# Attention and a SwiGLU FFN in one kernel: values loaded ahead of two q/k transfers, product pieces from unit 8, and a gate step in a small PSUM bank

## The chip, the cores and the metric

The kernel runs on one core of a Trainium2 chip. TensorE does matrix products into PSUM, ScalarE the exponentials, tanh and some evictions, VectorE the other element-wise work, GpSimd (POOL) issues most transfers and makes some copies, SyncE (SP) issues the rest. The metric is the device time of one execution in microseconds (us); below it is the median of eight executions.

## The reference, cut to what matters

Attention over 8 batches of 12 heads, 448 positions, head size 64. Its output, as 3584 tokens of 768, goes through a gated FFN of 1536 hidden units.

```python
scores = np.matmul(q, k.transpose(0, 1, 3, 2)) / np.sqrt(64)
scores = scores - np.max(scores, axis=-1, keepdims=True)
attn = np.exp(scores)
attn = attn / (np.sum(attn, axis=-1, keepdims=True) + 1e-09)
x = np.matmul(attn, v)            # then (B, S, H*D), flattened to 3584 x 768
g = x @ w_gate
silu = g * (1.0 / (1.0 + np.exp(-g)))
out = (silu * (x @ w_val)) @ w_out
```

## The kernel before

The unit of the attention is a pair of heads: 48 pairs, six to a batch. Each pair is cut into four chunks of 112 key positions. `qk` (line 215) makes the scores of one chunk for both heads in one two-bank tile of the pool `ps_s`, and ScalarE's exponential (line 227) takes them to the tile E. `pv_chunk` (line 237) adds one chunk's product of E and the values to the accumulator `acc`; the values carry a column of ones, so that the sum of the exponentials comes with it. After the fourth chunk VectorE takes the reciprocal (line 265) and scales into `xt` (line 266). `turn_x` (line 283) transposes `xt` into X, which the FFN reads: on TensorE for the pairs below 12 (lines 293 and 297, then VectorE's copy, line 304), by DMA for the later ones. For pairs 1 to 10 `prep` transposes q and k on TensorE (line 207), with VectorE's copies (lines 208 and 211); later pairs go through POOL copies (line 166) and DMA transposes.

PSUM has eight banks. `ps_s` has three tiles of two banks, used in turn for the scores, for the transposes of pairs below 8, and for the FFN's gate product `gp`. `ps_f` has two tiles of one bank, called small banks here, used in turn for `acc`, the transposes of pairs from 8 on, the turns of x from pair 6 on, the FFN's value product `vp`, its output product `op`, and dummies. A new tile takes the buffer that was allotted longest ago and waits until the last reader of that buffer is done.

An FFN step (`ffn1_steps`, line 313) is six matmuls of the gate weights, six of the value weights, a tanh (line 334), and two VectorE steps: line 339 reads `sg` and `gp`, line 342 reads `vp` and writes `hts`. Twelve steps make a block of tokens; then `ffn2_steps` multiplies with the output weights (line 365) and ScalarE evicts (line 372).

The order of the work on each engine is written by hand. The first stage (line 476) has 24 units u, one chunk of scores each, for pairs 0 to 5. A unit may also turn q and k (`prep`), run a dummy matmul, copy values, emit loads (`wq`), turn x, and run pieces: a piece is one `pv_chunk` of the list `pieces`, allowed where its chunk number is at most u - 3, and here only from unit 12 on. Pairs 6 to 47 follow in visits (line 528) of two, later three chunks of scores. A visit may have products of a whole pair (`todo`); one with scores but without products is called bare. Then come FFN steps, as many as a budget gives. Before them a flag is set in bare visits that have no output step to run first: `val_first` (lines 568 and 584) makes the next FFN step run its value product ahead of its gate product.

Each engine runs its instructions in order. Transfers on the POOL queue wait for the landing of the eighth transfer before them. Values are loaded for three pairs in one transfer at first (`load_v`, line 132; 336 KB), then copied to a layout with the column of ones (`copy_v`, line 139): on POOL for pairs 0 to 5, on VectorE after that. `load_qk16` (line 118) loads q and k as 16-bit numbers, two pairs at a time from pair 4 on.

Of the kernel before, what the change touches and what calls it, by code (L numbers as in the profile page):

```python
# [10 lines left out]
FP32 = mybir.dt.float32  # L11
# [7 lines left out]
GP = 3  # L19
# [3 lines left out]
FIRST = 6  # L23
# [4 lines left out]
NV = 6  # L28
VS = 6
# [4 lines left out]
def kernel(  # L34
# [10 lines left out]
    nc = tc.nc  # L45
    B, H, S, D = q.shape
# [3 lines left out]
    NC = S // P  # L50
# [29 lines left out]
    ps_s = ctx.enter_context(tc.tile_pool(name="ps_s", bufs=3, space=PSUM))  # L80
    ps_f = ctx.enter_context(tc.tile_pool(name="ps_f", bufs=2, space=PSUM))
# [3 lines left out]
    Vts = [consts.tile([P, 2, NC, D + 2], FP16, name=f"vo{i}") for i in range(NV)]  # L85
    vraw = consts.tile([P, VS, 2, NC, D], FP16, name="vraw")
# [7 lines left out]
    def wslice(kind, fb, cb):  # L94
        i, off = divmod(fb * 128, DF // 4)
        return wgv[kind, i][:, cb, ds(off, 128)]
# [7 lines left out]
    def dummy(n):  # L104
        wp = ps_f.tile([128, 512], FP32, tag="f", name="wp")
        for _ in range(n):
            nc.tensor.matmul(wp[:], lhsT=warm[:, 0:128], rhs=warm[:], start=True, stop=True)
# [10 lines left out]
    def load_qk16(pr, n=2):  # L118
        h0 = 2 * (pr % 2) if pr >= 14 else 0
        if h0 == 0:  # L120
            q16 = raws.tile([P, 4, NC, D], FP16, tag="rq", bufs=RB, name="q16")
            k16 = raws.tile([P, 4, NC, D], FP16, tag="rk", bufs=RB, name="k16")
            pairbuf[:] = [q16, k16]
        q16, k16 = pairbuf
        for dst, src in ((q16, q), (k16, k)):
            flat = src.rearrange("b h s d -> (b h) s d")[2 * pr : 2 * pr + 2 * n]
            nc.gpsimd.dma_start(dst[:, ds(h0, 2 * n)], flat.rearrange("h (p c) d -> p h (c d)", c=NC))  # L127
        for i in range(n):
            h = h0 + 2 * i
            raw[pr + i] = (q16[:, h : h + 2], k16[:, h : h + 2])  # L130

    def load_v(pr, n=1):
        b, h = divmod(2 * pr, H)
        nc.gpsimd.dma_start(  # L134
            vraw[:, ds(pr % VS, n)].rearrange("p r h c d -> p (r h) (c d)"),
            v[b, h : h + 2 * n].rearrange("h (p c) d -> p h (c d)", c=NC),
        )

    def copy_v(pr):
        eng = nc.gpsimd if pr < FIRST else nc.vector  # L140
        eng.tensor_copy(Vts[pr % NV][:, :, :, 0:D], vraw[:, pr % VS])  # L141

    def load_w(kind, i):
        if kind == "o":
# [134 lines left out]
    def pv(pr):  # L279
        for c in range(NC):  # L280
            pv_chunk(pr, c)
# [26 lines left out]
        )  # L308
        nc.sync.dma_start_transpose(dst[:, 0:D].rearrange("p (j q) -> p j q", j=1), xt[0:D, 3])

    val_first = [False]

    def ffn1_steps(kk, c0, n, hts):
        for fb in range(NFB):
            gp = vp = None

            def group(kind, dst):
                for cb in range(NCB):
                    nc.tensor.matmul(  # L319
                        dst[:, 0:n],  # L320
                        lhsT=wslice(kind, fb, cb),
                        rhs=X[kk][:, cb, ds(c0, n)],
                        start=(cb == 0),
                        stop=(cb == NCB - 1),
                    )

            if val_first[0]:
                val_first[0] = False
                vp = ps_f.tile([128, 512], FP32, tag="f", name="vp")
                group("v", vp)  # L330
            gp = ps_s.tile([128, 2, 512], FP32, tag="s", name="gp")[:, 0]
            group("g", gp)
            sg = fp.tile([128, 512], FP32, tag="sg")
            nc.scalar.activation(sg[:, 0:n], gp[:, 0:n], AF.Tanh, scale=0.5)  # L334
            if vp is None:
                vp = ps_f.tile([128, 512], FP32, tag="f", name="vp")
                group("v", vp)
            t1 = fp.tile([128, 512], FP32, tag="t1")
            nc.vector.scalar_tensor_tensor(  # L339
                t1[:, 0:n], sg[:, 0:n], 1.0, gp[:, 0:n], ALU.add, ALU.mult  # L340
            )
            nc.vector.scalar_tensor_tensor(  # L342
                hts[:, fb, 0:n], t1[:, 0:n], 0.5 * HS, vp[:, 0:n], ALU.mult, ALU.mult
            )
            yield
# [53 lines left out]
    with tc.manual_schedule():  # L399
# [7 lines left out]
        make_identity(nc, ident)  # L407
        load_qk16(2, 1)
        load_qk16(3, 1)
        load_qk16(4)  # L410
        load_v(0, GP)
        load_v(3, GP)
        dummy(7)
        prep(0)()
# [12 lines left out]
        def emit(item):  # L427
            if item[0] == "qk":
                load_qk16(*item[1:])
            elif item[0] == "V":  # L430
                load_v(item[1] * GP, GP)
            else:
                load_w(*item)
# [31 lines left out]
        def left():  # L465
            return sum(2 * t for _, t in fvq) + sum(t for _, t in oq)

        def share(total, at, n):
            return (at + 1) * total // n - at * total // n

        pieces = [(p, c) for p in range(FIRST) for c in range(NC)]

        def piece():
            pv_chunk(*pieces.pop(0))

        for u in range(FIRST * NC):
            pr, c = divmod(u, NC)
            qk(pr, c)
            if u == 1:
                dummy(1)  # L480
                turn()
                dummy(1)
            elif u == 3:
                dummy(2)
            elif u == 4:
                prep(2)()
            elif u >= 6 and c == 2:
                prep(pr + 2)()
            if u in (5, 7, 8, 9, 11):
                dummy(1)  # L490
            if c == 1:
                if pr in (1, 3):
                    for p in range(3):
                        copy_v(3 * (pr // 2) + p)
                for w in wq.pop(pr, []):
                    emit(w)
            if u in (15, 17, 19, 21):
                turn_x((u - 15) // 2)
            for _ in range(2):
                if u >= 12 and pieces[0][0] * NC + pieces[0][1] <= u - 3:  # L500
                    piece()

        queue = []
# [24 lines left out]
        for x, (chunks, todo) in enumerate(plan):  # L528
            for pr, c in chunks:
                qk(pr, c)  # L530
            end = min([y for y in adds if y > x] + [len(plan) + 1])
            if x == 0:
                piece()
                turn_x(4)
                piece()
                piece()
                turn_x(5)
                add_block(0, end)
            for p0 in vcopies.get(x, []):
                copy_v(p0)  # L540
            entered = [pr for pr, c in chunks if c == 0]
            for pr in entered:
                if NPE <= pr + 3 < NPAIR:
                    prep(pr + 3)
                if 14 <= pr + LA < NPAIR:
                    load_qk16(pr + LA, 1)
                if 12 <= pr + 3 < NPAIR:
                    load_v(pr + 3)
            for pr, c in chunks:
                if c == 2 and pr < NPE - 2:  # L550
                    prep(pr + 2)()
            if x in adds and x > 0:
                add_block(adds[x], end - x)
            for _, p0 in todo:
                pv(p0)
                if p0 < XPE:
                    turns.append(p0)
                else:
                    turn_x(p0)
            for pr in entered:  # L560
                for w in wq.pop(pr, []):
                    emit(w)
            bare = not todo and bool(chunks)
            if adds[max(y for y in adds if y <= x)] < 2:
                if bare and oq and not fvq:
                    carry -= run_o()
                elif bare:
                    val_first[0] = True
                carry = run_budget(left() / (end - x) + carry)
            else:  # L570
                at, n = count["at"], count["visits"]
                no = share(count["o"], at, n)
                nf = 1
                if no and count["more"] > 0:
                    o_left = sum(1 for y in range(at, n) if share(count["o"], y, n))
                    extra = -(-count["more"] // o_left)
                    nf += extra
                    count["more"] -= extra
                count["at"] += 1
                if bare and no:  # L580
                    run_o()
                    no -= 1
                elif bare:
                    val_first[0] = True
                for y in range(nf):
                    if fvq:
                        run_fv()
                for _ in range(no):
                    run_o()
            while turns:  # L590
                turn_x(turns.pop(0))
# [39 lines left out]
```

The softmax here doesn't subtract the row's maximum and nothing guards it: scores larger than these inputs give would overflow.

## Time and profile before

| what | value |
|---|---|
| median of 8 executions | 456.94 us (456.41 to 457.5) |
| profiled execution, device time | 457.12 us |
| its span, first to last instruction | 455.3 us |
| TensorE busy | 444.6 us |
| ScalarE, VectorE, POOL busy | 238.9, 200.4, 141.8 us |
| read from HBM, written | 47.19 MB, 11.01 MB |
| the FFN's first matmul starts | 33.10 us |

The chain that ended last is 92% TensorE: output product 24%, gate 24%, value 24%, probability products 10%, scores 8%. In the timeline a row gives start, duration, engine, line, operation, what is written and read, shapes and count; brackets give the idle time of that engine before the row and what ended it. Matmul rows overlap at their ends, because matmuls are pipelined, so distances between starts are better measures of what a group costs than durations. Line numbers are those of the kernel before. The waits list sums the same idle times by who waited for whom.

### The profile page before, as it was taken

Reading aid. Unit: us, or ns where it says so; the run is one execution under the profiler, and the core shown is the slowest. Engines: PE = TensorE matmul, PEld = TensorE weight load, DVE = VectorE, ACT = ScalarE, POOL = GpSimd, SP = SyncE. Lnnn points to the kernel's source line nnn. Section 1 sums busy time; section 2 is a strip of 40 time slices with the busy share of each in tenths; the row PEclk is TensorE's granted clock in tenths of the full one; section 3 lists DMA queues with packets and bytes.
Section 4 is the critical chain, followed back from the end, with each engine's and each line's share of the span. In section 5 each row is a group of like instructions: output and inputs, shape, how many; then the busy total and the mean of one; then the engine's idle time right before and its main releaser. Section 6 shows DMA issues by size and latency. Waiting matters only on the chain.

```text
span 455.3 us, 9850 instructions
## 1 busy us (share of the span) xinstructions
PE 444.6 (98%) x4009; PEld 247.8 (54%) x4009; DVE 200.4 (44%) x450; ACT 238.9 (52%) x350; POOL 141.8 (31%) x228
## 2 busy tenths in 40 slices
PE   8989999999999999999999999999999999999997
PEld 3555555645455656545455565555555556644464
DVE  3455653356563534363453544444355444245400
ACT  6865476765654546644556455654654644222222
POOL 8664805926344315251332503441100000000000
PEclk9999999999999999999999999999999999999999
DMA  9999999999685739784766837983423102110033
GB/s 130 197 200 202 184 179 161 188 199 120 97 105 85 108 76 149 109 118 93 122 81 106 132 70 125 141 94 68 71 61 77 46 13 79 47 36 0 1 106 104
DMA packets 104942, 48.72 MB, mean 107 GB/s; under 512 B 59584, under 2 KB 101440, under 8 KB 104896
## 3 DMA queue, kind: packets, MB, share of 16 engines
q0 software_dynamic: 43296, 23.37, 41.4%
q1 hardware_dynamic: 61504, 24.66, 27.3%
q8 instruction: 31, 0.51, 0.5%
q14 instruction: 15, 0.12, 0.1%
q10 hardware_dynamic: 96, 0.05, 0.0%
HBM read 47.19 MB, written 11.01 MB: 128 GB/s over the span
## 4 chain that ended last, share of the span: by engine, by line
PE 92%; DMA 3%; POOL 2%; DVE 1%; ACT 1%; issue 1%; POOLq 0%; DVEq 0%
PE op L365 24%; PE gp L319 24%; PE vp L319 24%; PE acc L245 8%; PE s L219 8%; DMA wg<-in_moe_w_gate_dram 3%; PE acc L253 2%; POOL q L127 1%; DVE t L339 1%; POOL k L127 1%; ACT sg L334 1%; PE tp L207 0%; ACT E L227 0%; POOL vraw L134 0%; PE acc L293 0%
## 5 line engine op out<-in xcount | busy, mean ns | idle before, releaser
L227 ACT ACTIVATE E<-s 112x896 f16<-112x896 f32 x192 | 162.4, 921 | 27.3 <-PE s L219 27.0
L319 PE MATMUL vp<-X,wv 128*128 128x384 f16 (+1 forms) x576 | 124.7, 353 | 0.0
L319 PE MATMUL gp<-X,wg 128*128 128x384 f16 (+1 forms) x576 | 124.5, 352 | 0.0
L365 PE MATMUL op<-wo,hts 128*128 128x384 f16 (+1 forms) x684 | 116.0, 323 | 0.0
L339 DVE SCALAR_TENSOR_TENSOR t<-sg,gp 128x384 f32<-128x384 f32 (+1 forms) x96 | 59.6, 621 | 123.4 <-ACT sg L334 123.3
L334 ACT ACTIVATE sg<-gp 128x384 f32<-128x384 f32 (+1 forms) x96 | 52.5, 547 | 90.5 <-PE gp L319 89.4
L365 PEld LDWEIGHTS <-hts 128*128 128x128 f16 x684 | 65.5, 98 | 45.9 <-issue 3.9
L319 PEld LDWEIGHTS <-wv 128*128 128x128 f16 x576 | 55.9, 98 | 52.9 <-issue 1.1
L319 PEld LDWEIGHTS <-wg 128*128 128x128 f16 x576 | 53.5, 98 | 45.3
L372 ACT ACTIVATE osb<-op 128x384 f32<-128x384 f32 (+1 forms) x57 | 27.8, 487 | 92.4 <-PE op L365 88.3
L166 POOL COPY qk<-q 112x512 f16<-112x512 f16 x37 | 23.0, 621 | 133.8 <-DMA qkT<-qk 132.3
L342 DVE SCALAR_TENSOR_TENSOR hts<-t,vp 128x384 f16<-128x384 f32 (+1 forms) x96 | 59.6, 620 | 10.8 <-PE acc L253 0.5
L245 PEld LDWEIGHTS <-E 112*128 112x128 f16 x1152 | 46.2, 97 | 17.1 <-issue 15.9
L219 PE MATMUL s<-qkT 64*128 64x448 f16 x384 | 51.2, 353 | 4.1 <-DVE t L339 3.1
L245 PE MATMUL acc<-vo,E 112*128 112x65 f16 x1152 | 52.6, 193 | 1.1 <-POOL vo L141 1.1
L253 PE MATMUL acc<-vo,E 112*128 112x65 f16 x384 | 42.9, 193 | 0.0
L265 DVE RECIPROCAL R<-acc 128x7 f32<-128x7 f32 x48 | 9.8, 205 | 73.7 <-PE acc L253 73.7
L134 POOL DMA_DIRECT2D vraw<-in_v_dram x40 | 26.7, 669 | 28.7 <-DVE vo L141 16.1
L219 PEld LDWEIGHTS <-qkT 64*128 64x128 f16 x384 | 15.2, 94 | 31.4 <-issue 24.6
L127 POOL DMA_DIRECT2D k<-in_k_dram x42 | 27.9, 664 | 9.6 <-PE gp L319 8.1
L127 POOL DMA_DIRECT2D q<-in_q_dram x42 | 28.1, 669 | 2.5 <-PE s L219 1.0
L266 DVE TENSOR_TENSOR xt<-acc,R 128x384 f16<-128x384 f32 (+1 forms) x48 | 27.5, 574 | 1.7
(43 smaller groups left out, 155.1 us busy)
## 6 DMA issues: line engine op xcount, KB each, us to landing
q<-in_q_dram POOLq DMA_DIRECT2D x37, 112.0 KB, 3.9
k<-in_k_dram POOLq DMA_DIRECT2D x37, 112.0 KB, 4.5
vraw<-in_v_dram POOLq DMA_DIRECT2D x36, 112.0 KB, 4.4
out_dram<-osb SPq DMA_DIRECT2D x7, 336.0 KB, 3.2
wg<-in_moe_w_gate_dram POOLq DMA_DIRECT2D x8, 288.0 KB, 11.2
wv<-in_moe_w_val_dram POOLq DMA_DIRECT2D x8, 288.0 KB, 11.7
wo<-in_moe_w_out_dram POOLq DMA_DIRECT2D x2, 1152.0 KB, 22.5
out_dram<-osb SPq DMA_DIRECT2D x8, 288.0 KB, 3.8
```

The costliest lines, as they stand in the source:

```text
L127: nc.gpsimd.dma_start(dst[:, ds(h0, 2 * n)], flat.rearrange("h (p c) d -> p h (c d)", c=NC))
L219: nc.tensor.matmul(s[:, hx, 0:S], lhsT=t[ts(hx, 64), c * P : c * P + 128], rhs=t[ts(hx, 64), ds(S + (1 - hx) * D, S)], start=True, stop=True,)
L227: nc.scalar.activation(e[:, :, 0:S], s[0:P, :, 0:S], AF.Exp, scale=sm_scale)
L245: nc.tensor.matmul(a7[:, 2 * j + hx], lhsT=e[:, ds(c * EB + 9 * hx + 2 * j, 2)].rearrange("p b x -> p (b x)"), rhs=vo[:, hx, c, 0 : D + 1] ...
L253: nc.tensor.matmul(a7[:, 6], lhsT=e[:, ds(c * EB + 6 + hx, 2)].rearrange("p b x -> p (b x)"), rhs=vo[:, hx, c, 0 : D + 1], start=False, st ...
L266: nc.vector.tensor_tensor(xt[:].rearrange("p j (h d) -> p (j h) d", h=2)[:, 0:n], a7[:, 0:n, 0:D], r[:, 0:n].unsqueeze(2).to_broadcast([12 ...
L319: nc.tensor.matmul(dst[:, 0:n], lhsT=wslice(kind, fb, cb), rhs=X[kk][:, cb, ds(c0, n)], start=(cb == 0), stop=(cb == NCB - 1),)
L334: nc.scalar.activation(sg[:, 0:n], gp[:, 0:n], AF.Tanh, scale=0.5)
L339: nc.vector.scalar_tensor_tensor(t1[:, 0:n], sg[:, 0:n], 1.0, gp[:, 0:n], ALU.add, ALU.mult)
L342: nc.vector.scalar_tensor_tensor(hts[:, fb, 0:n], t1[:, 0:n], 0.5 * HS, vp[:, 0:n], ALU.mult, ALU.mult)
L365: nc.tensor.matmul(op[:, 0:w], lhsT=hts[:, fb, ts(ch, 128)], rhs=wo[oh][:, fb, ds(m0 - oh * OH, w)], start=(fb == 0), stop=(fb == NFB - 1),)
L372: nc.scalar.activation(osb[:, ds(m0, w)], op[:, 0:w], AF.Copy, scale=1.0 / HS)
```

## The change

Values of pairs 0 to 2 are loaded before q and k of pairs 4 and 5. All copies of values run on VectorE; those of pairs 0 to 2 are in unit 6 (after its transposes), of pairs 3 to 5 in unit 14, where both sets stood on POOL in units 5 and 13. Dummies are left in units 5, 6 and 7. Pieces may run from unit 8 on; a unit with a transpose set (c == 2) or a turn of x runs one piece, others up to two. The turns of x for pairs 0 to 3 move from units 15, 17, 19, 21 to 11, 15, 17, 20. In the first visit the turn of pair 4 stands before all remaining pieces rather than after one of them.

In the bare visits the flag, now `gate_small`, no longer puts the value product first. Instead the gate product runs first as in other steps, but in a small bank of `ps_f` rather than in a tile of `ps_s`.

```diff
     def copy_v(pr):
-        eng = nc.gpsimd if pr < FIRST else nc.vector
-        eng.tensor_copy(Vts[pr % NV][:, :, :, 0:D], vraw[:, pr % VS])
+        nc.vector.tensor_copy(Vts[pr % NV][:, :, :, 0:D], vraw[:, pr % VS])
...
-            if val_first[0]:
-                val_first[0] = False
-                vp = ps_f.tile([128, 512], FP32, tag="f", name="vp")
-                group("v", vp)
-            gp = ps_s.tile([128, 2, 512], FP32, tag="s", name="gp")[:, 0]
+            if gate_small[0]:
+                gate_small[0] = False
+                gp = ps_f.tile([128, 512], FP32, tag="f", name="gp")
+            else:
+                gp = ps_s.tile([128, 2, 512], FP32, tag="s", name="gp")[:, 0]
             group("g", gp)
             sg = fp.tile([128, 512], FP32, tag="sg")
             nc.scalar.activation(sg[:, 0:n], gp[:, 0:n], AF.Tanh, scale=0.5)
-            if vp is None:
-                vp = ps_f.tile([128, 512], FP32, tag="f", name="vp")
-                group("v", vp)
+            vp = ps_f.tile([128, 512], FP32, tag="f", name="vp")
+            group("v", vp)
...
+        load_v(0, GP)
         load_qk16(4)
-        load_v(0, GP)
         load_v(3, GP)
...
+        XAT = (11, 15, 17, 20)
...
-            if u in (5, 7, 8, 9, 11):
+            if u in (5, 6, 7):
                 dummy(1)
+            if u in (6, 14):
+                for p in range(3):
+                    copy_v(u // 8 * 3 + p)
             if c == 1:
-                if pr in (1, 3):
-                    for p in range(3):
-                        copy_v(3 * (pr // 2) + p)
                 for w in wq.pop(pr, []):
                     emit(w)
-            if u in (15, 17, 19, 21):
-                turn_x((u - 15) // 2)
-            for _ in range(2):
-                if u >= 12 and pieces[0][0] * NC + pieces[0][1] <= u - 3:
+            if u in XAT:
+                turn_x(XAT.index(u))
+            for _ in range(1 if c == 2 or u in XAT else 2):
+                if u >= 8 and pieces[0][0] * NC + pieces[0][1] <= u - 3:
                     piece()
...
             if x == 0:
-                piece()
                 turn_x(4)
-                piece()
-                piece()
+                while pieces:
+                    piece()
                 turn_x(5)
...
-                    val_first[0] = True
+                    gate_small[0] = True
```

More of the change, by code (lines that the diff above doesn't have):

```diff
@@ L309, in turn_x @@
         nc.sync.dma_start_transpose(dst[:, 0:D].rearrange("p (j q) -> p j q", j=1), xt[0:D, 3])
-    val_first = [False]
+    gate_small = [False]
     def ffn1_steps(kk, c0, n, hts):
         for fb in range(NFB):
-            gp = vp = None
             def group(kind, dst):
@@ L583 @@
                 elif bare:
-                    val_first[0] = True
+                    gate_small[0] = True
                 for y in range(nf):
```

## The prediction

> **What bounds the kernel now.** I read the page's busy line, then the waits, then the timeline of each engine around the places that the waits name.
>
> ```profile
> PE 444.6 (98%) x4009; PEld 247.8 (54%) x4009; DVE 200.4 (44%) x450; ACT 238.9 (52%) x350; POOL 141.8 (31%) x228
> PEclk9999999999999999999999999999999999999999
> ```
> ```profile
> PE s L219 <- DVE t L339: 3.1, 4, 0.9
> PE acc L245 <- POOL vo L141: 1.1, 2, 1.0
> PE acc L293 <- DVE xt L266: 1.0, 1, 1.0
> ```
>
> TensorE is busy 98% of the span. Time can only come from its gaps or from instructions it no longer has. The gaps named are 3.1 us of score products waiting for a gate bank (line 339 frees it), and about 2 us in the first stage. After 123 us the waits show no TensorE gap, so whatever is gained or lost before that reaches the end one for one.
>
> The four gaps, and the second FFN visit with what VectorE does meanwhile (start, duration, engine):
>
> ```profile
> 38.17 1.14 PE L319 MATMUL vp<-X,wv 128*128 128x384 f16 x6
> 39.14 1.14 PE L319 MATMUL gp<-X,wg 128*128 128x384 f16 x6
> 40.21 0.55 PE L219 MATMUL s<-qkT 64*128 64x448 f16 x4
> ...
> 50.40 0.36 PE L219 MATMUL s<-qkT 64*128 64x448 f16 x2 [0.68 <-DVE t L339]
> ...
> 60.46 0.37 PE L219 MATMUL s<-qkT 64*128 64x448 f16 x2 [0.61 <-DVE t L339]
> 60.76 0.35 PE L245 MATMUL acc<-vo,E 112*128 112x65 f16 x6
> ...
> 100.19 0.37 PE L219 MATMUL s<-qkT 64*128 64x448 f16 x2 [0.92 <-DVE t L339]
> 100.49 0.35 PE L245 MATMUL acc<-vo,E 112*128 112x65 f16 x6
> ```
> ```profile
> 38.73 0.29 DVE L141 COPY vo<-vraw 112x512 f16<-112x512 f16 x1 [0.61 <-DMA vraw<-in_v_dram]
> 38.94 0.62 DVE L208 COPY qkT<-tp 128x896 f16<-128x896 f16 x1
> 39.47 0.18 DVE L211 COPY qkT<-tp 128x64 f16<-128x64 f16 x1
> ...
> 46.99 0.72 DVE L141 COPY vo<-vraw 112x512 f16<-112x512 f16 x1
> ```
>
> At 38.73 VectorE had stood 0.61 us for the values of pair 6, and pair 8's turned q and k (lines 208, 211) stood behind that copy until 39.65. Nobody was hurt then: the next user of that bank came at 40.70.
>
> The values of pair 6 and the queue that brings them:
>
> ```profile
> 28.11 0.77 POOL L134 DMA_DIRECT2D vraw<-in_v_dram  x1 [0.42 <-issue]
> vraw<-in_v_dram POOLq DMA_DIRECT2D x1, 336.0 KB, 10.5
> 20.00:24.00 4.00, 3.30 (x69) 2.35 (x66) 3.19 (x8) 2.96 (x4) 2.59 (x4) 1.00 1.32 203
> 32.00:36.00 4.00, 3.33 (x23) 2.06 (x24) 1.46 (x3) 0.75 (x2) 2.18 (x4) 1.00 1.44 197
> ```
>
> Issued at 28.11, landed 10.5 later, at 38.6. The last two lines are four-microsecond stretches: busy time of TensorE, its weight loads, VectorE, ScalarE and POOL, then granted clock, DMA share and GB/s. The queue moves 195 to 203 GB/s in every 4 us stretch from 12 to 44 us, so a landing there is a matter of bytes ahead of it, not of when it is issued. The change swaps two transfers early on and adds none: pair 6 stays at 38.6.
>
> **Part 1: first stage (values first, VectorE copies, pieces from unit 8, fewer dummies).** The last transfer ahead of the swapped ones lands at 10.8 (k of pair 3, issued 5.25). The two value loads then took 1.8 and 2.3 us (landings 13.6, 15.4, 17.7), so values of pairs 0 to 2 come near 12.8 and k of pairs 4 and 5 near 15.4, where values came before. Six copies leave POOL (0.61 each) and cost VectorE 0.28 each where nothing disturbs them. TensorE per unit, from the starts in the timeline: scores 0.29, a lone piece 0.35, two pieces 0.57, a transpose set 0.52, a turn of x 0.42. Unit 8 starts at 12.3 as before (a score bank sets it), its pieces at about 13.1 with the copy; unit 10 stands for k until 15.4; unit 12 starts near 17.1 where before it was 15.55, but with six pieces and one turn done. Units 12 to 23 then hold 3 x 0.87 (two pieces) + 3 x 1.16 (transposes and a piece) + 3 x 1.06 (a turn and a piece) + 3 x 0.64 = 11.2, ending at 28.3 against 29.9. The tail (scores, turn 4, three pieces, normalisation, turn 5) keeps its 0.95 us stall before turn 5, merely elsewhere, and the FFN starts at about 31.7 instead of 33.1: 1.4 us earlier. The two lost dummies (0.3 each) lie in the stretch that the score bank sets, and are worth nothing alone.
>
> **Part 2: the second FFN visit eats it.** The bare visits (no probability products) run value first before, with gate in the three-deep score banks. Now gate takes a small bank, then value the other. The small banks are two and rotate: in this visit the transposes of pair 8 take one, gate the other, and value needs the transposes' bank back. That is line 211's end, 39.65, fixed by the landing at 38.6. Before, value took the older bank and gate a score bank, so neither waited. Now value starts at 39.70, however early TensorE arrives (37.7, after gate), and everything else on TensorE queues behind it. The next scores start a group and its tail later, 39.70 + 1.07 = 40.77 against 40.21: **+0.56**, and the 1.4 us are gone. The stage's result therefore doesn't matter over a wide range: it would have to end 0.56 us later than before to add anything, and no earlier end helps.
>
> **Part 3: the other bare visits.** Now the third score product needs only an exponential of the visit before. Its ungapped start is two pitches of 0.19 after the first.
>
> Visit at 47: the third score pair could start at 49.54 instead of 50.40, worth 0.86. Against it: value waits for the transposes of pair 9, whose copies ended at 48.32 on VectorE while value would start at 48.09: 0.28. That copy stood behind a value copy that took 0.72 (46.99) where the same copy takes 0.28 elsewhere (57.50), with POOL writing transfers until 47.59 and then copying:
>
> ```profile
> 45.54 2.05 POOL L154 DMA_DIRECT2D wo<-in_moe_w_out_dram  x2 [1.19 <-issue]
> 47.57 0.63 POOL L166 COPY qk<-q 112x512 f16<-112x512 f16 x1
> 48.12 0.63 POOL L166 COPY qk<-k 112x512 f16<-112x512 f16 x1
> ```
>
> With TensorE 0.56 later this copy comes at 47.55 and meets the POOL copies. Bounds of the wait: 0 if it takes 0.28; 1.1 if it stands until 48.75. Nearest is the row's own 0.28; I take 0.40. Net **-0.46**.
>
> Visit at 57: the scores flow, but the accumulator now needs the gate's bank, freed by line 339. The tanh stands behind three exponentials in both versions, so line 339 ends at 60.41 as before; the accumulator starts at 60.46 against 60.76: **-0.30**. The wait has moved, not gone.
>
> Visits at 96 and 118: gate is now done before the exponentials are, so the tanh follows them at once: 95.81 + 2.43 = 98.24, tanh 0.60, line 339 (0.69) from 98.87 to 99.56, accumulator at 99.61 against 100.49: **-0.88**. The same steps from 118.42 give 122.22 against 123.15: **-0.93**.
>
> Sum: +0.56 - 0.46 - 0.30 - 0.88 - 0.93 = -2.0. The profiled execution took 457.12 (span 455.3 and 1.8 around it), so 455.1; it stands 0.18 over the median of the eight, so **454.9**. Unknowns: pair 6's landing, one for one, up to one transfer of 1.14 us either way (26.4 to 27.6, values that pair with a 224 KB load); the 0.40, from 0 to 1.1.
>
> A rule that speaks against the change: the Trainium skill, "SBUF — State Buffer", section "SBUF: two separate sides", says that VectorE's fast copies and GpSimd lock each other out of a shared pair of ports for a whole instruction, and that transfers issued from GpSimd suffer because their descriptors can't be written. The 0.72 row agrees in kind. Six more such copies on VectorE would lock some 1.7 us, and were pair 6 as much later the time would be 456.6 by an estimate from that page; by the queue's steady rate, none of it.
>
> **The rivals.**
> *The gain of the first stage arrives* (faster). It needs pair 6 by 36.7, or value not to depend on it. Then -1.4 replaces +0.56: -3.97, **453.0**. For it: most of the edit is made there. Against: the steady 200 GB/s.
> *The wait takes the place of the one removed* (same). If the accumulator stands for the value's bank (line 342) rather than the gate's, then 60.51 + 0.55 gives 61.11 (+0.35), and 0.10 + 0.69 after line 339 gives 100.40 and 123.01 (-0.09, -0.14): sum +0.22, **457.2**. For it: in the visit at 47 the accumulator does follow the value's bank. Against: the banks rotate, and elsewhere the older one is the gate's.
> *TensorE's clock falls in units 8 to 12* (slower). Dummies go while TensorE waits for values at unit 8 and for k at unit 10. Place: the 15.2 us of work of units 8 to 23. It decides only beyond 2.0 us of slack before 39.70, 2.0 of later gains and 0.9: a mean clock under 15.2 / 20.1 = 0.76. At 0.65 it costs 8.2, **461**. Against: the stretches at 20 and 32 us hold gaps of 0.97 and 0.96 and show 1.00. The Trainium skill, "TensorE: Matmul & The Clock Gate", section "What's actually happening", has the clock halve only after an idle window of some 3.4 us; halving all units would give 468 by that page, and the rows show no such idleness.
>
> **How the numbers follow.** Forecast 0.66, with its own range 453.8 to 456.1; faster rival 0.12; same rival 0.12; slower 0.10. Half of the same rival and the slower one are left out by 453.0 to 456.5. A measurement can tell 0.2%, 0.9 us: faster means under 456.03, slower over 457.85. Of the forecast's 0.66 some 0.03 falls within: faster 0.63 + 0.12 = 0.75, same 0.12 + 0.03 - 0.01 = 0.14, slower 0.11.
>
> **What would show it.** Right: FFN starts near 31.7; a TensorE gap of about 2 us before value at 39.7, released by VectorE's copy of pair 8's transposes; a landing of pair 6 at 38.6; a gap of about 0.55 before the accumulator at 60; gaps under 0.3 near 99 and 122; no score product waiting for line 339 at the four places. Wrong: pair 6 landing elsewhere; a score product still waiting at those places; a clock below 1.00; a new wait after 123 us.

## The result, and the profile after

The changed kernel takes 454.16 us (median of 11, 453.76 to 455.38) where the kernel before took 456.85 beside it: ratio 0.9939, 95% interval 0.9930 to 0.9948, that is 2.4 to 3.2 us less. The forecast was 2.0 less. The profiled execution took 453.57, 0.6 under that median, with a span of 451.8, against 457.12 and 455.3. In three of the four sets of experiments below, two or three executions of the kernel before took 461.4 to 461.8 at a mean granted clock of 0.988 or 0.989, which makes the ratios there up to 0.2% smaller than the medians would.

From here on line numbers are those of the kernel in whose profile they stand; in the changed kernel the scores are line 218, the probability products 244 and 252, gate and value 317, the gate's VectorE step 336, the copies of values 140, of transposes 207 and 210.

The page's head and, from its waits, all rows in which TensorE waited for VectorE in matmuls of scores, products and turns (who, for whom, us in all, times, longest):

```profile
span 451.8 us, 9845 instructions
PE 443.7 (98%) x4007; PEld 247.1 (55%) x4007; DVE 201.5 (45%) x456; ACT 239.4 (53%) x350; POOL 138.4 (31%) x222
```
```profile
PE acc L292 <- DVE xt L265: 1.3, 2, 1.0
PE acc L244 <- DVE t L336: 0.5, 1, 0.5
PE acc L244 <- DVE X L303: 0.3, 1, 0.3
PE s L218 <- DVE qkT L195: 0.3, 1, 0.3
```

The row of 3.1 us, scores waiting for the gate's step, is gone. In its place stands one of 0.5, the accumulator of the visit at 57. The third row is new too: a product of the first stage waits for VectorE's copy of a turn. The last stands in the kernel before as well. TensorE's busy time is 0.9 us less (443.7 against 444.6). Two dummies of 0.39 are gone; what else makes up the difference isn't shown.

TensorE at the bare visits of the changed kernel (start, duration, what, and in brackets the idle time before):

```profile
37.09 1.15 PE L317 MATMUL gp<-X,wg 128*128 128x384 f16 x6
38.33 1.15 PE L317 MATMUL vp<-X,wv 128*128 128x384 f16 x6
39.41 0.55 PE L218 MATMUL s<-qkT 64*128 64x448 f16 x4
...
48.36 0.74 PE L218 MATMUL s<-qkT 64*128 64x448 f16 x6
...
57.57 0.74 PE L218 MATMUL s<-qkT 64*128 64x448 f16 x6
58.80 0.34 PE L244 MATMUL acc<-vo,E 112*128 112x65 f16 x6 [0.49 <-DVE t L336]
...
96.74 0.74 PE L218 MATMUL s<-qkT 64*128 64x448 f16 x6
97.63 0.34 PE L244 MATMUL acc<-vo,E 112*128 112x65 f16 x6
```

Three score pairs run as one group of six where the group used to break after four. VectorE in the second visit and in the one at 47:

```profile
37.35 0.29 DVE L140 COPY vo<-vraw 112x512 f16<-112x512 f16 x1 [0.40 <-DMA vraw<-in_v_dram]
37.56 0.62 DVE L207 COPY qkT<-tp 128x896 f16<-128x896 f16 x1
38.09 0.18 DVE L210 COPY qkT<-tp 128x64 f16<-128x64 f16 x1
46.19 0.28 DVE L140 COPY vo<-vraw 112x512 f16<-112x512 f16 x1
```

VectorE stood for the values of pair 6, the copies of pair 8's transposes stood behind, and TensorE's value product came at 38.33, 0.06 after line 210: the chain that was forecast. But the values landed at 37.33, not at 38.6, so TensorE stood 0.10 there (0.26 by the starts: 1.24 from gate to value, where 0.98 is usual) and not 2.0.

Where the time came from, as the start of each visit's probability products against the kernel before: 39.90 for 40.70, 49.55 for 51.21, 58.80 for 60.76, 97.63 for 100.49, 119.33 for 123.15. The distance is -0.80, -1.66, -1.96, -2.86, -3.82, and stays: the last matmul ends at 448.24 against 452.07. Of these 3.8 us 0.3 are lost again after the last matmul (see the padded kernel below).

### The profile page after: what moved, and what is told of

It reads as the page before. It is cut to its first block, busy times and chain, and to the rows that moved or that the text cites. A ratio compares the mean times of both kernels' runs of the same rounds, so it can differ in the third digit from the quotient of the medians.

```text
span 451.8 us, 9845 instructions
## 1 busy us (share of the span) xinstructions
PE 443.7 (98%) x4007; PEld 247.1 (55%) x4007; DVE 201.5 (45%) x456; ACT 239.4 (53%) x350; POOL 138.4 (31%) x222
## 4 chain that ended last, share of the span: by engine, by line
PE 90%; DMA 4%; DVE 2%; ACT 2%; POOL 1%; issue 1%; DVEq 0%; ACTq 0%; POOLq 0%
PE op L362 24%; PE gp L317 23%; PE vp L317 22%; PE acc L244 8%; PE s L218 8%; DMA vraw<-in_v_dram 4%; PE acc L252 2%; ACT E L226 1%; DVE t L336 1%; PE tp L206 1%; ACT sg L332 1%; POOL k L127 0%; DVE qkT L207 0%; POOL q L127 0%; DVE vo L140 0%
## 5 line engine op out<-in xcount | busy, mean ns | idle before, releaser
L134 POOL DMA_DIRECT2D vraw<-in_v_dram x40 | 26.7, 669 | 29.6 <-DVE vo L140 17.1
L127 POOL DMA_DIRECT2D k<-in_k_dram x42 | 27.8, 663 | 10.7 <-PE vp L317 7.8
```

## The experiments

Times are medians; each set ran beside the kernel before (456.8 to 457.3), and the ratio is to that, with its 95% interval. Edits are against the changed kernel; `...` marks what is left out.

### Each half of the change alone

The first takes the first stage of the changed kernel and the FFN step of the kernel before; the second the other way round.

```diff
 # stage only: the FFN step keeps the old order
+            if val_first[0]:
+                val_first[0] = False
+                vp = ps_f.tile([128, 512], FP32, tag="f", name="vp")
+                group("v", vp)
...
 # bank only: loads, copies, dummies, pieces and turns as before
-        load_v(0, GP)
         load_qk16(4)
+        load_v(0, GP)
...
```

> The first-stage half of the change alone; bare visits run the value product first in the old way. Theory (the second FFN visit takes the stage's gain only because its value product waits for the bank of pair 8's transposes): here value takes the older bank, so the earlier FFN start of 1.0 us (32.1 against 33.1 in the profile of the changed kernel) arrives at the end: 455.9, with the four score waits on line 339 still there (3.1 us in the waits). Rival A (the loads' queue sets the pace and the stage is worth nothing): 456.9. Rival B (the stage is where most of the gain comes from): 454.9 or less.

> The small gate bank alone; the first stage as before. Theory: the second visit's value starts about 1.0 us after the landing of pair 6's values, between 38.4 and 39.7, against its natural 39.1, so 0 to +0.6 there; then -0.86, -0.30, -0.88, -0.93 in the four later bare visits: 453.9 to 454.6. Rival A: the same. Rival B: the waits only move, 456.2 or more.

The stage alone took 456.98, ratio 0.9990 (0.9965 to 1.0015): not to be told from the kernel before. The bank alone took 454.32, ratio 0.9922 (0.9895 to 0.9950). So the gain is the bank's, as the sum of the prediction had it. But the theory's 455.9 for the stage missed; the time was that of rival A. The waits of the stage-only kernel:

```profile
PE s L218 <- DVE t L338: 3.1, 4, 0.9
PE acc L292 <- DVE xt L265: 1.3, 2, 1.0
```

The four waits on the gate's step are all there, as they must be. What failed was the size of the stage's gain: in this execution the values of pairs 0 to 2 landed at 13.26, unit 8 stood 0.68 us for them, and the FFN began at 32.78, only 0.32 before the old 33.10. That 0.32 did reach the last matmul (451.76 against 452.07), against rival A, and was then lost behind the last matmul, where the span ends 3.54 later and not 3.25. Seven profiles of the same first stage, in this and later runs, have the FFN start between 32.08 and 32.78.

The bank alone lies within its forecast of 453.9 to 454.6. Its value product of the second visit started at 39.20, right behind the gate product, with the landing at 37.97, and the accumulators came at 40.76, 50.66, 59.90, 98.73 and 120.43: steps of -0.61, -0.31, -0.90 and -0.96 in the four later visits.

### Is it the landing?

In one kernel VectorE's copy of the next values goes behind the transposes' copies; in the others the load of pairs 6 to 8 moves, later by two weight transfers or earlier by two of q and k.

```diff
 # copy behind
-            for p0 in vcopies.get(x, []):
-                copy_v(p0)
...
                 if c == 2 and pr < NPE - 2:
                     prep(pr + 2)()
+            for p0 in vcopies.get(x, []):
+                copy_v(p0)
 # later
-            3: [("qk", 10), ("V", 2), ("g", 2), ("v", 2)],
+            3: [("qk", 10), ("g", 2), ("V", 2), ("v", 2)],
 # earlier
+            3: [("V", 2), ("qk", 10), ("g", 2), ("v", 2)],
```

> The changed kernel, with VectorE's copy of the next pair's values moved behind the copies of the transposed q and k in each visit. Theory: the value product of the second visit no longer hangs on the landing of pair 6; stage and banks add up, -1.0 - 2.97 = -4.0: 452.9, and the gap before value in the second visit is under 0.1 us whatever the landing. Rival A (the queue sets the pace anyway, through the products of pair 6): 454.2, the time of the changed kernel. Rival B: 454.2.

> The changed kernel with the values of pairs 6 to 8 loaded two gate-weight transfers later (1.45 us each). Theory: landing at 40.2 to 41.5, value of the second visit about 1.0 us after that, one for one to the end: 454.2 + 2.9 = 457.1. Rival B (the landing does not matter): 454.2.

> The changed kernel with the values of pairs 6 to 8 loaded before q and k of pairs 10 and 11 (two transfers of 1.15 us). Theory: landing about 2.3 us earlier, 35.0 to 36.3, no wait before the second visit's value; what is left is the stage (0.3 to 1.0) and the four later visits (2.97): 3.3 to 4.0 under the kernel before, that is 0.5 to 1.2 under the repeated changed kernel. Rival (landing immaterial in its usual place): within 0.3 of the repeated changed kernel.

> The changed kernel once more, beside the next three. Theory (value of the second visit starts 1.0 us after the landing of pair 6's values, or when TensorE arrives, whichever is later): 2.8 us under the kernel before, as first measured, and in its profile the start of that value product fits one of the two; the landing may differ by half a microsecond from the 37.3 of the first profile. Rival (landing immaterial): the gap before that value product is 0.1 us again at any landing.

Later: 459.50, ratio 1.0033 (1.0007 to 1.0058), slower than the kernel before. VectorE and TensorE of that kernel in the second visit:

```profile
41.15 0.29 DVE L140 COPY vo<-vraw 112x512 f16<-112x512 f16 x1 [4.04 <-DMA vraw<-in_v_dram]
41.36 0.62 DVE L207 COPY qkT<-tp 128x896 f16<-128x896 f16 x1
41.90 0.18 DVE L210 COPY qkT<-tp 128x64 f16<-128x64 f16 x1
```
```profile
42.13 1.15 PE L317 MATMUL vp<-X,wv 128*128 128x384 f16 x6 [3.74 <-DVE qkT L210]
43.21 0.92 PE L218 MATMUL s<-qkT 64*128 64x448 f16 x4
44.06 0.51 PE L244 MATMUL acc<-vo,E 112*128 112x65 f16 x6
```

Landing 41.13, value at 42.13. With 37.33 and 38.33 in the first profile and 37.73 and 38.74 in the repeat (wait 0.15), value is at landing plus 1.0 in all three, one for one: the mechanism is shown. The loss was bigger than forecast, though. The span grew by 5.3 us over the first profile, the landing only by 3.80. The score and product groups above are slow (0.92 for 0.55, 0.51 for 0.34). Stretches of that kernel (busy time of TensorE, its loads, VectorE, ScalarE, POOL; then the granted clock, the DMA share and GB/s):

```profile
42.00:44.00 2.00, 1.87 (x10) 0.63 (x10) 1.09 (x3) 0.14 (x1) 1.17 (x2) 0.82 1.31 202
44.00:46.00 2.00, 2.00 (x35) 1.89 (x34) 0.00 (x0) 1.58 (x2) 0.98 (x1) 0.50 1.33 209
46.00:48.00 2.00, 2.00 (x12) 1.09 (x10) 0.90 (x3) 0.49 (x1) 2.00 (x4) 0.83 1.31 195
```

After 3.74 us without a matmul the granted clock was 0.50 for some 3.4 us (2 us times 0.36, 1.00 and 0.34 of the time), and the visits there lost 1.57 us more. The times agree: the two of the twelve executions with a mean granted clock of 1.00 took 457.30 and 457.90, near the forecast 457.1; the ten others, at 0.989 to 0.996, took 458.19 to 460.45.

Earlier: 453.98, ratio 0.9940 (0.9928 to 0.9953); the repeat beside it: 454.46, 0.9947 (0.9935 to 0.9960). Landing 35.31, and no wait before value, as the theory said; but the times can't be told apart, since there had only been 0.15 us of standing to save (0.32 by the starts), and the visit at 47 gave 0.32 back, where the next value copy took 0.73 us instead of 0.28. In the usual place the rival has the size right: the landing is near to mattering, and hardly does.

Copy behind: 453.82, ratio 0.9916 (0.9888 to 0.9944). Landing 38.03; TensorE's second visit in that profile runs through:

```profile
37.60 1.15 PE L317 MATMUL gp<-X,wg 128*128 128x384 f16 x6
38.58 1.14 PE L317 MATMUL vp<-X,wv 128*128 128x384 f16 x6
39.65 0.55 PE L218 MATMUL s<-qkT 64*128 64x448 f16 x4
```

Value comes 0.55 after the landing, so the dependence is cut. Half a microsecond is as much as it would have cost here; the 1.3 between the forecast 452.9 and the changed kernel's 454.2 isn't shown, and against the bank alone in the same set (454.32) it can't be told.

### More of the same, and the gate between two scores

```diff
 # combined: copy behind, pair 6 early, and
-        load_v(0, GP)
-        load_qk16(4)
+        load_v(0)
+        load_qk16(4, 1)
+        load_v(1, 2)
+        load_qk16(5, 1)
...
-            if u in (6, 14):
-                for p in range(3):
-                    copy_v(u // 8 * 3 + p)
+            for p in {6: (0,), 9: (1, 2), 13: (3, 4, 5)}.get(u, ()):
+                copy_v(p)
 # gate between: the same, and in the bare visits near 57, 96, 118
+                if early and n == 2:
+                    gate_small[0] = True
+                    spent = run_fv()
                 qk(pr, c)
...
```

> Copies of the next values behind the transposes' copies and pair 6 early, both as before; then in the first stage the values of pair 0 alone go first, q and k of pair 4 next, values of pairs 1 and 2, q and k of pair 5; copies in units 6, 9 and 13. Theory: values of pair 0 land near 11, unit 8 no longer waits (0.1 to 0.7 in the profiles), the 0.3 us that the first product of pair 3 waited is gone, and all of it arrives: 4.3 to 4.7 under the kernel before. Rival (the queue of loads takes the stage's gain back further on): 3.3 to 4.0 under, with a new TensorE gap after 33 us.

> The same, and in the bare visits near 57, 96 and 118 the FFN step stands between the second and the third chunk of scores, so that the tanh is behind two exponentials and not three. Theory: the accumulators' waits on line 336 (0.49, 0.15, 0.09) go, 0.5 to 0.7 us under the kernel of the row before. Rival (the wait moves to the gate's bank or to the exponentials): no difference.

> The combined kernel once more. Its first profile had TensorE's clock released at 10.5 us where the others had 4.2 to 6.0, and its FFN began 1.3 us later than that of the kernel with the same first stage. Theory (that was one execution's accident): release near 5.5, FFN start near 31.9, median near 453.0. Rival (the late release belongs to this kernel): release near 10 again, 454.1.

The combined kernel took 454.08, ratio 0.9934 (0.9921 to 0.9948): the rival's time. But its profile shows no new gap after 33 us, and pair 0 landed at 10.49 with no wait at unit 8, as the theory said; the FFN nevertheless began at 33.11. The dummies of the first units tell why, first in the combined kernel and then in the one with the same first stage:

```profile
5.55 0.61 PE L107 MATMUL wp<-warm 128*128 128x512 f16 x1
7.09 0.61 PE L107 MATMUL wp<-warm 128*128 128x512 f16 x1
8.52 0.61 PE L107 MATMUL wp<-warm 128*128 128x512 f16 x1
```
```profile
5.48 0.39 PE L107 MATMUL wp<-warm 128*128 128x512 f16 x1
6.71 0.39 PE L107 MATMUL wp<-warm 128*128 128x512 f16 x1
7.55 0.39 PE L107 MATMUL wp<-warm 128*128 128x512 f16 x1
```

The same matmul took 0.61 until past 8 us in one execution and 0.39 from 5 us in the other, whose FFN began at 31.79. Run again, the combined kernel took 452.60, ratio 0.9882 (0.9841 to 0.9924), with the FFN at 31.89. So the late start does not belong to the kernel. It was hardly one execution's alone, for four of the five in the first set took 454.05 to 454.15. The same code has medians 1.5 us apart in two sets of runs, on two chips, and differences of that size between sets aren't read here.

Gate between: 454.42, ratio 0.9946 (0.9934 to 0.9959), no gain. The wait moved, as its rival said, to the exponential of the third scores, which now starts late. First the waits' row, then the first of the three places:

```profile
PE s L218 <- ACT E L226: 2.0, 3, 0.7
58.30 0.36 PE L218 MATMUL s<-qkT 64*128 64x448 f16 x2 [0.63 <-ACT E L226]
```

By the traces this is a loss: against the combined kernel's second profile, whose FFN began at 31.89 where this one's began at 31.79, the accumulator of the visit at 118 comes 1.60 us later (120.47 for 118.87).

### Filling the stall before the turn of pair 5

```diff
-                qk(pr, c)
+                if x != 1:
+                    qk(pr, c)
...
                 while pieces:
                     piece()
+                for pr, c in plan[1][0]:
+                    qk(pr, c)
+                prep(FIRST + 2)()
                 turn_x(5)
...
-                if c == 2 and pr < NPE - 2:
+                if c == 2 and FIRST < pr < NPE - 2:
                     prep(pr + 2)()
...
-                    gate_small[0] = True
+                    gate_small[0] = x > 1
```

> The combined kernel with the stall of 0.96 before the turn of pair 5 filled: the second visit's scores and pair 8's transposes are issued before that turn, the first two visits keep gate in a score bank, and the turn of pair 3 is in unit 21. Theory (a TensorE gap before 37 us is worth its size once the second visit hangs on no landing): 0.9 to 1.2 under the combined kernel, 5.0 to 5.5 under the kernel before. Rival (gains before the second visit are taken back by later loads): within 0.3 of the combined kernel, 2.5 to 3.3 under, with a new gap between 37 and 60 us.

> The changed kernel with only the fill: the second visit's scores and pair 8's transposes ahead of the turn of pair 5, gate in a score bank in the first two visits. The transposes' copies then stand ahead of VectorE's copy of pair 6's values, so nothing in the second visit waits for the landing; the products of pair 6 do, but their landing (37.3 to 38.0, copy 0.3) is about when TensorE comes (38.3 to 39.3). Theory: 0.9 to 1.3 under the changed kernel, 3.7 to 4.1 under the kernel before. Rival (the combined kernel's other edits are needed for it): within 0.3 of the changed kernel.

On top of the combined kernel this took 451.37 (451.22 to 451.50), ratio 0.9867 (0.9837 to 0.9898): the fastest here, clear of the changed kernel's 0.9930 to 0.9948. TensorE where the stall of 0.96 used to stand:

```profile
29.98 0.55 PE L218 MATMUL s<-qkT 64*128 64x448 f16 x4
30.46 0.39 PE L206 MATMUL tp<-ident,q 112*64 112x112 f16 x8
30.68 0.36 PE L206 MATMUL tp<-ident,k 112*64 112x112 f16 x8
31.01 0.34 PE L292 MATMUL acc<-ident,xt 128*128 128x128 f16 x3
```

No idle time is left before the turn. The products of pair 6 begin at 38.01, 1.33 before those of the kernel with the same loads and a like clock (39.34), which is the forecast 0.9 to 1.2 and a little. Its median is 2.7 under that of the combined kernel's first set and 1.2 under that of its second; both are other sets, so the trace is the better measure. On the changed kernel alone the fill took 453.51, ratio 0.9911 (0.9883 to 0.9938); the forecast 3.7 to 4.1 less lies in that interval (2.8 to 5.3), and so nearly does the changed kernel's 2.7. Its profile had the slow first units as well (FFN at 33.66) and shows the stall gone. So the fill is shown in the trace and in the combined kernel, not by the time of the fill alone.

### The lost 0.3 at the end

> The changed kernel with six tiny POOL memsets where the six POOL copies used to be. In the profiles of kernels with six fewer POOL instructions the span ends 3.55 us after TensorE's last matmul, in the others 3.25. Theory (the end depends on where POOL's last instructions lie in its program): 3.25 here. Rival (the end depends on the copies or on VectorE): 3.55.

```diff
                 for p in range(3):
                     copy_v(u // 8 * 3 + p)
+                    nc.gpsimd.memset(pad[:], 0.0)
```

TensorE's last group, of the kernel before (span 455.3) and of the changed one (span 451.8):

```profile
442.78 9.29 PE L365 MATMUL op<-wo,hts 128*128 128x384 f16 x68
```
```profile
439.76 8.48 PE L362 MATMUL op<-wo,hts 128*128 128x384 f16 x63
```

It ends at 452.07 and at 448.24, 3.25 and 3.56 before the end of the span. With the six memsets it is 3.31 (448.74 of 452.05; one execution, 453.83). The copies stayed on VectorE, so it is not they. Over all the profiles the stretch goes with the number of POOL's instructions: 3.54 to 3.57 in the seven profiles with 222 of them, 3.25 to 3.31 in the seven with 225 or 228, of which the four of the combined, the gate-between and the filled combined kernels have their copies on VectorE too. What it is about their number or place isn't shown.

## Why the prediction was right, point by point

The direction and the part that brings the gain were right: the two halves alone show that the small bank brings it and the first stage none that can be measured. The size (2.0 forecast, 2.4 to 3.2 measured) was right in part by luck. The loss that the second visit was to bring did not come, and the gain at 47 was larger than forecast; 0.3 at the end was not in the sum. With the terms as measured the sum is -3.5 and -3.1 in the two profiles of the changed kernel, and these executions took 3.5 and 3.1 less than the profiled one of the kernel before; the medians are only 2.7 and 2.3 apart.

- First stage, -1.4: -1.0 in the first profile, -0.3 to -0.9 in the others with the same stage. The copies after 12.6 and the 0.96 before the last turn came as worked out. The wait for k at unit 10 did not: k landed at 14.93 and its transposes began at 14.97, 0.05 later than they could have behind those of q, so unit 12 began at 16.71 and not at 17.1. Units 12 to 23 then took 12.0 and not 11.2, with two waits that the sum did not have: 0.32 of a product for a bank behind the copies of unit 14, and 0.30 before the turn of pair 3. The size hangs on one landing: the values of pairs 0 to 2 came between 12.4 and 13.3 in the seven profiles, and the FFN began 19.5 to 19.8 after that.
- Second visit, +0.56: the mis-sized term. The step was "pair 6 stays at 38.6". It landed between 37.3 and 38.0 in six later profiles with its load in the old place (38.96 in one with late first units), so value started close behind gate and the term was -0.80 and -0.40 in two profiles of the changed kernel. One profile's landing was taken for a constant to a tenth, from the steady rate. The rate was as steady again (within 2 GB/s of the old one in each stretch from 12 to 44 us), but it does not fix a landing: when pair 6 landed, the queue had moved 6.39 MB in the kernel before and 6.16 MB in the changed one. Nor did the landing part from the issue, as the prediction had it: from 28.11 to 38.64 before, from 26.81 to 37.33 after, 10.5 to 10.7 apart in all eight profiles with the load in that place; the issue itself waits for an earlier landing. What makes a landing come earlier isn't shown. The prediction allowed 1.14 either way; the first profile's was 1.31 early, the five others 0.6 to 0.9.
- "The 1.4 us are gone", "the stage's result doesn't matter": with the wait at 0.10 to 0.15 (0.26 and 0.32 by the starts) this fell. The stage gets through; it is small by itself.
- Visit at 47, -0.86 and a wait of 0.40: -0.86 and -0.85 in two profiles of the changed kernel, with no wait. In the bank-only kernel it was -0.61 with that copy at 0.65, and with pair 6 early -0.53 with the copy at 0.73; in the first two the copy took 0.28. POOL's work beside it is not the whole reason: in the changed kernel POOL copied from 46.26 on, and VectorE's copy at 46.19 took 0.28 all the same.
- Visits at 57, 96 and 118, -0.30, -0.88, -0.93: measured -0.30, -0.90, -0.96 in both profiles. The rows of before gave these to a few hundredths, because ScalarE's order and the rotation of banks fix them.
- Not in the sum: +0.3 at the end.

As for the rivals: the wait at the later visits did not grow to the size of the one removed, since the accumulators wait for the gate's step and not for the value's. The granted clock did not fall in units 8 to 12 (1.00 in the stretches from 10 to 16). The gain of the first stage did pass the second visit, as far as there was one: -1.02 at the FFN's start became -0.80 in one profile of the changed kernel, and -0.66 became -0.40 in the other.

## What to carry to other kernels

A bank that is taken in turn ties its next user to the last reader of its previous tile, and through that reader's queue to whatever the reader's engine waits for; walk that chain for every user that a change adds to a pool, and put copies that wait for a landing behind those that free a bank. A tile freed early is worth what the next wait leaves: here the scores gained 0.86 to 1.09 of running time, and the accumulator's wait took up to 0.6 of it back. A landing read from one profile is good to about a microsecond, so a term that hangs on it is a range.

## What the runs showed of the hardware that was not expected

- The clock at the start rises at a time that the kernel does not set. In one execution of the combined kernel the 512-column dummies took 0.61 up to 9.92 us, the trace's first record of the granted clock (1.00) stands at 10.51, and the FFN began at 33.11. In another the dummies took 0.39 from 6.86 on, the record stands at 6.74, and the FFN began at 31.89. Over the fourteen profiles that record lies between 4.14 and 10.51. (The page's PEclk row shows 1.00 ahead of it too, so the lengths of the dummies are the better sign.)
- A gap of 3.74 us on TensorE brought the granted clock to 0.50 (in the trace from 43.26, 1.1 us after the work went on, to 46.68); gaps up to 0.97 left it at 1.00, and behind the start no profile has one in between. This agrees with the Trainium skill, "TensorE: Matmul & The Clock Gate", section "What's actually happening", which puts the idle window at about 3.4 us; the low stretch here was 3.4 us too.
- Copies of values on VectorE varied beside POOL's work. The six that came over from POOL took 0.70 and 0.69 us by threes in the changed kernel, with POOL issuing weight transfers around them; in two other profiles of the same first stage the second three took 0.82 and 0.93. Single copies take 0.28 where nothing disturbs them; one took 0.72 beside the issue of the output weights (before, at 46.99), one 0.93 beside an issue and POOL's copies (changed kernel, at 81.45), one 1.38 beside POOL's copies (its repeat, at 105.12). The 0.28 at 46.19 shows that not every copy beside POOL is slow; what decides isn't shown.
